# Thirteen transposes per head instead of fifteen: a new order of 64-blocks in the raw q/k tiles of an attention-and-mixing kernel

## The chip, the cores and the metric

One core of one Trainium2 chip runs the whole program. The metric is device time in microseconds (us), as the median of three runs. A profile of one further execution gives the trace from which all rows below are taken.

## The reference, cut to what matters

```python
B, H, S, D = 4, 8, 576, 64            # 32 heads of 576 positions, 64 wide
scores = (1 / sqrt(D)) * q @ k.T      # float32
cum    = cumsum(maximum(s, 0.0))      # one row of 576 per head
bias   = -(cum[:, None] - cum[None, :])
scores = where(causal, -1e9, scores + minimum(bias, 0.0))
attn   = softmax(scores)
x      = attn @ v                     # heads side by side: (4, 576, 512)
gate   = sigmoid(causal convolution of x, 5 taps)
x      = (gate * (x @ w_val)) @ w_out
h      = relu(x @ w_in);  u, v = halves of h, 512 wide each
v_n    = layer norm of v
out    = (u * (w_spatial @ v_n + b_spatial)) @ w_out2
```

q, k, v and s are float32; the weights come as 64-bit floats and are converted on the chip.

## The kernel before, in words

**Heads.** The main loop (L678 to L718) runs over rounds `w` of 0 to 32. Round `w` computes the scores of head `w`, turns the exponentials of head `w-1` and, when `w` is even, multiplies the pair of heads `w-2` and `w-1` with their values (`pv`). The first 8 heads (`NATIVE`) use plain float32 matmuls for the scores; the later ones split q and k into a high and a low part (`prep`) and use the faster float32r form.

**Scores.** The 576 queries of a head are cut into five tiles: 64 queries (positions 0 to 63) and four of 128. Tile `i` is scored against the keys up to its last query, so it has 64, 192, 320, 448 or 576 columns (`QE`). `scores` puts a tile's product in a PSUM bank; VectorE adds the mask and takes the row minimum of the negated scores (L219, into `p[i]`); ScalarE takes the exponential in place and sums the rows (L224). The last tile exceeds a bank of 512 columns and is cut into 288 and 288. Each of the five tiles has an SBUF tile of its own, `p[0]` to `p[4]`, and there are two sets.

**Turns.** The product with the values needs the exponentials with the keys on the partitions, so TensorE turns blocks of 128 queries by 128 keys with an identity as the moving operand (L271), into banks of up to five turns, and ScalarE copies each bank to `PT` (L272). There are 15 blocks on or under the diagonal; five of them, the last of each query tile (`c == i`), hold only 64 keys, and their turn fills half of its 128 columns' worth. The banks are `BANKS[0]` to `BANKS[3]` with 5, 1, 4 and 5 turns, and a round turns them in the order 1, 2, 3, 0 (L691, L699, L704).

**Values.** `pv` multiplies both heads of a pair; each head's product stands on its own 64 partitions of the bank. The six products of a head take 448, 448, 320, 192, 64 and 128 columns, 1600 in all. VectorE scales the result by the reciprocal row sums (L300), which were turned, written to DRAM and read back spread over partitions (`lay_sums`, `spread_sums`). `conv` then forms the gate's input.

**Mixing.** Beside the heads a queue of generators (`more`) feeds in weight conversion (`from_f64`, `weight_prep`, `fold_prep`), the folding of two weights, and the mixing stages of batches already attended. `n_g` sets how much of it each round takes, in five portions. The mixing of the last batch stands alone after the last head.

**Transfers.** All loads are issued from SP's queue, in the order of its instructions; an instruction that waits holds those behind it. `load(h)` brings q and k of a head (one transfer, L147 for the first 8 heads, L150 for the others), for the first 8 heads the row `cum` (L148), and the values (L152). `raw` has two buffers, `vraw` four. The same queue loads weights (L369, L471), the `cum` rows of the later heads (L168), a copy of q (L170) and the row sums (L248).

**Order.** The order of instructions on each engine is drawn up by the framework's planner from the program order and its own estimates; only a few places are pinned by hand.

Of the kernel before, what the change touches and what calls it, by code (L numbers as in the profile page):

```python
# [15 lines left out]
NEG = -1.0e30  # L16
# [8 lines left out]
def tile_stickbreak_attention_moe(  # L25
# [30 lines left out]
    BANKS = [[(4, 4), (1, 1), (1, 2), (1, 3), (1, 4)], [(0, 0)], [(0, 1), (0, 2), (0, 3), (0, 4)],  # L56
             [(2, 2), (2, 3), (2, 4), (3, 3), (3, 4)]]
    BLK, w = {}, 0
    for bank in BANKS:
        for c, i in bank:  # L60
            BLK[c, i] = w
            w += 64 if c == i else 128
    PTW = w
# [28 lines left out]
    V.memset(RAW[0][64:65, 0, :], 1.0)  # L92
    G.memset(RAW[1][64:], 0.0)
    G.memset(RAW[1][64:65, 0, :], 1.0)
# [6 lines left out]
    for c in (0, 128):  # L101
# [3 lines left out]
    mask = early.tile([128, S], F32, name="mask")  # L105
    G.memset(mask, 0.0)
    G.affine_select(out=mask[:, S - 128:], in_=mask[:, S - 128:], compare_op=ALU.is_ge, fill=NEG,
                    base=0, pattern=[[-1, 128]], channel_multiplier=1)
# [11 lines left out]
    for j in range(2):  # L120
        P.append([early.tile([128, e + 64], F32, name=f"p{j}{i}") for i, e in enumerate(QE)])
        for t, e in zip(P[j], QE):
            G.memset(t[:, e:], 0.0)
        G.memset(P[j][0][64:], 0.0)
# [16 lines left out]
    def load(h, cum=None):  # L141
        if h >= NH:
            return
        raw[h] = r = RAW[h % 2]
        src = qk2[h].rearrange("p (t s) -> p t s", t=2)
# [10 lines left out]
    def prep(h):  # L156

        if h >= NH:
            return
        r = raw.pop(h)  # L160
        if h < NATIVE:
            st[h] = r
            return
        qk = early.tile([128, 2, S], F32R, tag="qk", name="qk", bufs=2)
        kd = kds[h % 2]
        qc = cn[h % 2]
        qa, kb = qk[:, 0, :], qk[:, 1, :]
        SY.dma_start(f(kd[64:66]), cum_d[h])  # L168
        hi_of(A, qa, r[:, 0, :])
        SY.dma_start(f(qc[0:64]), f(qa[0:64]))  # L170
        lo_of(V, qa[64:128], r[64:128, 0, :], qa[64:128])
        hi_of(A, kb, r[:, 1, :])
        lo_of(V, kd[0:64], r[0:64, 1, :], kb[0:64])
        st[h] = (qa, kb, qc, kd)
# [15 lines left out]
    def scores(h, tiles):  # L190
        if h >= NATIVE:
            qa, kb, qc, kd = st[h]
        p = P[h % 2]
        if h not in NM:
            NM[h] = early.tile([128, 6], F32, tag="nm", name="nm", bufs=2)
        nm = NM[h]
        parts = []
        pst = None
        o = 0
        for i in tiles:  # L200
            q0, m, e = QS[i], QM[i], QE[i]
            spans = [(0, e)] if e <= 512 else [(0, HS), (HS, e)]
            for a, b in spans:
                if pst is None or o + b - a > 512 or len(spans) > 1:
                    pst = room("s", "pss", h)
                    o = 0
                if h < NATIVE:
                    r = st[h]
                    T.matmul(pst[0:m, o:o + b - a], r[:, 0, q0:q0 + m], r[:, 1, a:b], start=True, stop=True)  # L209
                else:  # L210
                    T.matmul(pst[0:m, o:o + b - a], qa[:, q0:q0 + m], kb[:, a:b], start=True, stop=False)  # L211
                    T.matmul(pst[0:m, o:o + b - a], qc[0:KD, q0:q0 + m], kd[0:KD, a:b], start=False, stop=True)  # L212
                parts.append((i, pst[0:m, o:o + b - a], a, b, len(spans)))
                o += b - a
        for i, src, a, b, n in parts:
            m, e = QM[i], QE[i]
            last = b == e
            o = S - max(e, 128) + a
            LAST["V"] = V.tensor_tensor_reduce(  # L219
                out=p[i][0:m, a:b], in0=src, in1=mask[0:m, o:o + b - a], scale=-0.125,  # L220
                scalar=3.0e38 if a == 0 else nm[0:m, 5:6], op0=ALU.add, op1=ALU.min,
                accum_out=nm[0:m, i:i + 1] if last else nm[0:m, 5:6])
            if last:
                A.activation(p[i][0:m, 0:e], p[i][0:m, 0:e], AF.Exp, bias=nm[0:m, i:i + 1], scale=-1.0,  # L224
                             accum_out=sm[h // 2 % 2][0:m, h % 2, i:i + 1])
# [31 lines left out]
    def transposes(h, tiles):  # L257

        p = P[h % 2]
        if h not in PT:  # L260
            PT[h] = early.tile([128, PTW], F32, tag="pt", name="pt", bufs=2)
        for bank in tiles:
            o0 = BLK[BANKS[bank][0]]
            pt = room("t", "pst", h)
            for c, i in BANKS[bank]:
                o = BLK[c, i]
                end = o + (64 if c == i else 128)


                r = 64 if c == i > 0 else 0  # L270
                T.transpose(pt[:, o - o0:o - o0 + 128], p[i][:, c * 128:(c + 1) * 128], ident[:, r:r + 128])  # L271
            A.activation(PT[h][:, o0:end], pt[:, 0:end - o0], AF.Copy)  # L272
# [3 lines left out]
    def pv(h):  # L276
# [3 lines left out]
        r = R.pop(h // 2).rearrange("p i q -> p (i q)")  # L280
        pts = [PT.pop(h + j) for j in range(2)]
        vs = [vraw.pop(h + j) for j in range(2)]

        first = None
        for tag, q0, q1 in (("o", 128, S), ("q", 0, 128)):
            po = ps.tile([128, 512], F32, tag=tag, name=f"ps{tag}", bufs=1)
            cs = [1, 0, 2, 3, 4] if q0 else [0]
            for c in cs:
                a = max(q0, c * 128)
                o = BLK[c, c] + a - c * 128  # L290
                for j in (1, 0):
                    with ExitStack() as es:
                        if first is not None:
                            es.enter_context(tc.issue_after(first))
                        m = T.matmul(po[64 * j:64 * j + 64, a - q0:q1 - q0], vs[j][:, c, :], pts[j][:, o:o + q1 - a],  # L295
                                     start=c == cs[0], stop=c == cs[-1])
                    first = first or m.ins
            for a, e in ((q0, 64), (64, q1)) if q0 == 0 else ((q0, q1),):
                o = a + 64 if a else 0
                V.tensor_tensor(out=x[:, a:e], in0=po[:, a - q0:e - q0], in1=r[:, o:o + e - a], op=ALU.mult)  # L300
# [22 lines left out]
    V.tensor_tensor_scan(out=cum, data0=s_sb, data1=s_sb, initial=0.0, op0=ALU.add, op1=ALU.max)  # L323
# [354 lines left out]
    for w in range(NH + 1):  # L678
# [11 lines left out]
        if w > 0:  # L690
            transposes(w - 1, [1, 2])  # L691
# [6 lines left out]
        if w > 0:  # L698
            transposes(w - 1, [3])  # L699
# [3 lines left out]
        if w > 0:  # L703
            transposes(w - 1, [0])  # L704
# [71 lines left out]
```

## Time and profile before

| | |
|---|---|
| median of 3 runs | 520.51 us (520.43 to 523.75) |
| the profiled execution | 523.57 us |
| its span, first to last instruction | 521.8 us |
| mean granted TensorE clock | 0.977 of full speed |
| TensorE matmul busy | 492.2 us, 94% of the span |
| ScalarE, VectorE busy | 339.3 us, 316.9 us |

The profiled execution's time is its span and 1.8 us around it. It stands 3.06 us above the median. PE is TensorE's matmul stream, PEld its weight loads, DVE VectorE, ACT ScalarE, POOL GpSimd, SP the queue of transfers. A matmul's recorded duration overlaps that of the next, so the step from one to the next is read from starts.

### The profile page before, as it was taken

The page shows a single profiled execution, that of the slowest core. Times are in us where ns is not written, and L with a number is a line of the kernel's source. Part 1 is how long each engine was busy: PE and PEld are TensorE (multiplying, and loading weights), DVE is VectorE, ACT ScalarE, POOL GpSimd, SP SyncE. Part 2 cuts the span into 40 slices and gives each one's busy share as a digit, 9 for nine tenths or more (in the row PEclk, how much of TensorE's full clock was granted, in tenths as well). Part 3 has the DMA queues.
Part 4 walks back from the last instruction along what each step waited for, and adds up shares of the span by engine and source line. Part 5 has one row for each costly group of instructions (what it writes and reads, how often), then busy time and mean ns, then how long its engine had stood idle before and what let it go on. Part 6 is the DMA issues. An engine that isn't in the chain of part 4 may idle for free.

```text
span 521.8 us, 9108 instructions
## 1 busy us (share of the span) xinstructions
PE 492.2 (94%) x3202; PEld 416.1 (80%) x3202; DVE 316.9 (61%) x834; ACT 339.3 (65%) x819; POOL 127.6 (24%) x167
## 2 busy tenths in 40 slices
PE   7889798989999999899999999999998999999997
PEld 5456564878769888889949889888878888998997
DVE  6778799788888684733748456744876526025120
ACT  3997797797687775864537647795869644224322
POOL 5212120036350103102235013003233013046140
PEclk9889798999999999989999999999998999999999
DMA  7839845356751643266511302666500052800002
GB/s 210 272 101 263 282 152 193 107 179 213 231 187 41 196 136 109 65 218 208 171 57 38 128 26 84 179 217 186 176 26 15 26 202 77 241 2 1 1 2 90
DMA packets 28302, 69.26 MB, mean 133 GB/s; under 512 B 4000, under 2 KB 12352, under 8 KB 28256
## 3 DMA queue, kind: packets, MB, share of 16 engines
q1 hardware_dynamic: 23328, 63.88, 39.7%
q10 hardware_dynamic: 4928, 4.80, 2.7%
q8 instruction: 25, 0.41, 0.3%
q14 instruction: 21, 0.17, 0.1%
HBM read 55.96 MB, written 9.16 MB: 125 GB/s over the span
## 4 chain that ended last, share of the span: by engine, by line
PE 65%; DVE 14%; DMA 10%; ACT 7%; issue 3%; SPq 1%; POOL 1%; ACTq 0%; DVEq 0%; POOLq 0%
PE psm L409 11%; PE psm L411 11%; PE psm L410 11%; PE pso L295 7%; PE pst L271 6%; PE psm L581 3%; DVE p L219 3%; PE psm L583 3%; PE psm L582 3%; PE pss L211 2%; DVE z L312 2%; PE pss L212 2%; DMA wr<-in_w_out 2%; PE pss L209 2%; DMA wv<-wo_d 1%
## 5 line engine op out<-in xcount | busy, mean ns | idle before, releaser
L224 ACT ACTIVATE p<-p,nm 64x64 f32<-64x64 f32 (+4 forms) x160 | 88.5, 555 | 10.5 <-DVE nm L219 10.0
L271 PE MATMUL pst<-ident,p 128*128 128x128 f32 x480 | 83.1, 284 | 7.3 <-ACT pt L272 3.8
L272 ACT ACTIVATE pt<-pst 128x512 f32<-128x512 f32 (+1 forms) x128 | 61.4, 496 | 34.2 <-PE psq L295 19.9
L219 DVE CUSTOM_DVE_ANT_0 p<-pss,mask 64x64 f32<-64x64 f32 (+4 forms) x160 | 64.1, 419 | 23.7 <-PE pss L212 17.1
L271 PEld LDWEIGHTS pst<-ident,p 128*128 128x128 f32 x480 | 61.5, 146 | 19.3 <-ACT pt L272 5.3
L312 DVE SCALAR_TENSOR_TENSOR z<-x,cw,z 128x575 f32<-128x575 f32 (+1 forms) x64 | 57.1, 892 | 6.2 <-ACT z L309 5.6
L79 POOL TENSOR_TENSOR g<-gt,g 128x288 fp32r<-128x288 f32 x32 | 29.2, 918 | 127.5 <-ACT g L72 95.2
L79 POOL TENSOR_TENSOR y<-gt,y 128x288 fp32r<-128x288 f32 x32 | 27.6, 867 | 111.1 <-ACT y L72 111.1
L295 PE MATMUL pso<-pt,vraw 128*64 128x448 f32 (+3 forms) x320 | 51.0, 431 | 1.2 <-ACT pt L272 1.2
L211 PE MATMUL pss<-qk 128*64 128x64 f32 (+1 forms) x144 | 45.2, 334 | 1.6 <-DVE nm L219 1.4
L295 PEld LDWEIGHTS pso<-pt,vraw 128*64 128x64 f32 x320 | 22.9, 139 | 27.0 <-issue 19.4
L212 PE MATMUL pss<-kd,cn 66*64 66x64 f32 (+1 forms) x144 | 42.1, 299 | 1.1 <-DVE kd L79 1.1
L209 PE MATMUL pss<-raw 128*128 128x288 f32 (+4 forms) x96 | 33.6, 453 | 7.0 <-DVE nm L219 5.3
L409 PE MATMUL psm<-g,wch 128*128 128x288 f32 x128 | 39.0, 310 | 0.2 <-ACT v L533 0.2
L581 PE MATMUL psm<-wsh,vh 128*128 128x288 f32 x128 | 38.5, 305 | 0.6 <-DVE gt L486 0.6
L411 PE MATMUL psm<-g,wch 128*128 128x288 f32 x128 | 38.5, 305 | 0.0
L410 PE MATMUL psm<-g,wcl 128*128 128x288 f32 x128 | 38.1, 302 | 0.0
L582 PE MATMUL psm<-wsh,vl 128*128 128x288 f32 x128 | 37.6, 298 | 0.0
L583 PE MATMUL psm<-wsl,vh 128*128 128x288 f32 x128 | 37.6, 297 | 0.0
L486 DVE TENSOR_TENSOR gt<-psm,u 128x288 f32<-128x288 f32 x32 | 14.4, 455 | 35.0 <-PE psm L585 22.1
L486 DVE TENSOR_TENSOR gt<-psm,z 128x288 f32<-128x288 f32 x32 | 14.4, 453 | 31.8 <-PE psm L411 29.2
L409 PE MATMUL psm<-y,wv 128*128 128x288 f32 x96 | 29.7, 310 | 3.8 <-ACT ot L596 2.9
(166 smaller groups left out, 1330.8 us busy)
## 6 DMA issues: line engine op xcount, KB each, us to landing
raw<-in_qk SPq DMA_DIRECT2D x24, 576.0 KB
wv<-wv_d SPq DMA_DIRECT2D x12, 512.0 KB
wv<-wo_d SPq DMA_DIRECT2D x12, 512.0 KB
vraw<-in_vp SPq DMA_DIRECT2D x32, 160.0 KB
R<-r_d SPq DMA_DIRECT2D x32, 160.0 KB
out<-ot ACTq DMA_DIRECT2D x32, 144.0 KB
cn<-qk SPq DMA_DIRECT2D x24, 144.0 KB
wr<-in_w_in SPq DMA_DIRECT2D x5, 512.0 KB
```

The lines of the kernel that those rows point to most:

```text
L79: eng.tensor_tensor(out=out_, in0=in_, in1=f(hi), op=ALU.subtract)
L211: T.matmul(pst[0:m, o:o + b - a], qa[:, q0:q0 + m], kb[:, a:b], start=True, stop=False)
L219: LAST["V"] = V.tensor_tensor_reduce(out=p[i][0:m, a:b], in0=src, in1=mask[0:m, o:o + b - a], scale=-0.125, scalar=3.0e38 if a == 0 else n ...
L224: A.activation(p[i][0:m, 0:e], p[i][0:m, 0:e], AF.Exp, bias=nm[0:m, i:i + 1], scale=-1.0, accum_out=sm[h // 2 % 2][0:m, h % 2, i:i + 1])
L271: T.transpose(pt[:, o - o0:o - o0 + 128], p[i][:, c * 128:(c + 1) * 128], ident[:, r:r + 128])
L272: A.activation(PT[h][:, o0:end], pt[:, 0:end - o0], AF.Copy)
L295: m = T.matmul(po[64 * j:64 * j + 64, a - q0:q1 - q0], vs[j][:, c, :], pts[j][:, o:o + q1 - a], start=c == cs[0], stop=c == cs[-1])
L312: V.scalar_tensor_tensor(out=z[:, d:], in0=x[:, :S - d], scalar=cw[:, p, k:k + 1], in1=z[:, d:], op0=ALU.mult, op1=ALU.add)
L409: T.matmul(pt, ah, bh, start=j == 0, stop=False)
L410: T.matmul(pt, al, bh, start=False, stop=False)
L411: T.matmul(pt, ah, bl, start=False, stop=j == n - 1)
L581: T.matmul(o, vh[c][:, cs], wsh[:, c, hs[hf]], start=c == 0, stop=False)
```

## The change

The keys of a head are laid in `raw` in another order: positions 512 to 575 first, then 0 to 511. The queries stand as 0 to 447, 512 to 575, 448 to 511. With it the five score tiles lie side by side in one SBUF tile of 1664 columns per set, and a half-filled block stands beside another half-filled block: the diagonal blocks of tiles 1 and 0 are turned together, and so are the last block of tile 3 and the first of tile 4. That leaves 13 turns per head, in four banks of 4, 4, 3 and 2.

What goes with it: `load` issues three transfers for q and k in place of one, in pieces of 1792, 256 and 256 bytes per row in place of one piece of 4608; the values come in two transfers, the second of which puts two blocks of 64 rows on the upper 64 partitions; the mask has 832 columns and four triangles instead of 576 and one; the scan that forms `cum` is cut in two; the last score tile is cut into 256 and 320; banks are turned in the order 3, 2, 0, 1; the value products take 512, 320, 192, 64, 448 and 64 columns, of which the two of 64 contract over the upper 64 partitions alone.

```diff
+    PO = [192, 0, 256, 640, 1088]
+    PW = 1664
+    MO = [384, 320, 192, 64, 0]
+    BANKS = [[(0, 0), (256, 0), (640, 0), (1152, 64)], [(128, 0), (384, 0), (768, 0), (1280, 64)],
+             [(512, 0), (896, 0), (1408, 64)], [(1024, 0), (1536, 64)]]
+    PTO = [(0, 0, 512), (512, 0, 512), (1024, 64, 320), (1344, 0, 256)]
...
-            SY.dma_start(r[0:64], src[0:64])
-            SY.dma_start(r[64:65, 1, :], one_d[h:h + 1] if cum is None else cum[h:h + 1])
-        else:
-            SY.dma_start(r, src)
-        vraw[h] = early.tile([128, 5, D], F32, tag="vraw", name="vraw", bufs=4)
-        SY.dma_start(vraw[h], vp[h].rearrange("p (c d) -> p c d", c=5))
+        by = r[0:n].rearrange("p t s -> p (t s)")
+        SY.dma_start(by[:, 64:1088].rearrange("p (t s) -> p t s", t=2)[:, :, 0:448], src[:, :, 0:448])
+        by = by.rearrange("p (g c) -> p g c", c=64)
+        SY.dma_start(by[:, 0:17:16], src[:, :, 512:])
+        SY.dma_start(by[:, 8:18:9], src[:, :, 448:512])
+        if h < NATIVE:
+            SY.dma_start(r[64:65, 0, :], one_d[h:h + 1] if cum is None else cum[h:h + 1])
+        vraw[h] = early.tile([128, 6, D], F32, tag="vraw", name="vraw", bufs=4)
+        vh = vp[h].rearrange("p (c d) -> p c d", c=5)
+        SY.dma_start(vraw[h][:, 0:4], vh[:, 0:4])
+        SY.dma_start(vraw[h][64:128, 4:], vh[0:64, 0::4])
...
-            spans = [(0, e)] if e <= 512 else [(0, HS), (HS, e)]
+            spans = [(0, e)] if e <= 512 else [(0, 256), (256, e)]
...
-            for c, i in BANKS[bank]:
...
-                T.transpose(pt[:, o - o0:o - o0 + 128], p[i][:, c * 128:(c + 1) * 128], ident[:, r:r + 128])
-            A.activation(PT[h][:, o0:end], pt[:, 0:end - o0], AF.Copy)
+            for t, (o, way) in enumerate(BANKS[bank]):
+                T.transpose(pt[:, 128 * t:128 * t + 128], p[:, o:o + 128], ident[:, way:way + 128])
+            to, o, n = PTO[bank]
+            A.activation(PT[h][:, to:to + n], pt[:, o:o + n], AF.Copy)
...
+        parts = [(0, 0, po), (2, 1024, po[:, 192:]), (3, 1408, po[:, 320:]), (4, 1344, po[:, 448:]),
+                 (1, 576, po[:, 64:]), (5, 512, pq)]
...
-    V.tensor_tensor_scan(out=cum, data0=s_sb, data1=s_sb, initial=0.0, op0=ALU.add, op1=ALU.max)
+    V.tensor_tensor_scan(out=cum[:, 64:], data0=s_sb[:, 0:512], data1=s_sb[:, 0:512], initial=0.0, op0=ALU.add, op1=ALU.max)
+    V.tensor_tensor_scan(out=cum[:, 0:64], data0=s_sb[:, 512:], data1=s_sb[:, 512:], initial=cum[:, S - 1:], op0=ALU.add,
+                         op1=ALU.max)
...
-            transposes(w - 1, [1, 2])
+            transposes(w - 1, [3, 2])
...
-            transposes(w - 1, [3])
+            transposes(w - 1, [0])
...
-            transposes(w - 1, [0])
+            transposes(w - 1, [1])
```

## Rows read from the trace of the kernel before

**Rows 1.** The page: busy time, share of span and instructions of each engine.

```profile
PE 492.2 (94%) x3202; PEld 416.1 (80%) x3202; DVE 316.9 (61%) x834; ACT 339.3 (65%) x819; POOL 127.6 (24%) x167
```

**Rows 2.** Busy time by stretch of the span, granted clock, DMA share and GB/s.

```profile
core 0: us, PE busy (x) PEld busy (x) DVE busy (x) ACT busy (x) POOL busy (x), PEclk, DMA share, GB/s
0.00:100.00 100.00, 85.13 (x425) 56.78 (x425) 81.20 (x232) 78.00 (x201) 23.39 (x40) 0.91 0.66 205
100.00:430.00 330.00, 319.64 (x2173) 275.38 (x2172) 210.88 (x558) 232.11 (x556) 77.47 (x92) 0.99 0.43 131
```

**Rows 3.** The chain that ended last, by line, whole span.

```profile
PE psm L409 11%; PE psm L411 11%; PE psm L410 11%; PE pso L295 7%; PE pst L271 6%; PE psm L581 3%; DVE p L219 3%; PE psm L583 3%; PE psm L582 3%; PE pss L211 2%; DVE z L312 2%; PE pss L212 2%; DMA wr<-in_w_out 2%; PE pss L209 2%; DMA wv<-wo_d 1%
```

**Rows 4.** Costliest groups, shapes apart: the turns; shares are busy us, mean ns.

```profile
L271 PE MATMUL pst<-ident,p 128*128 128x128 f32 x480 | 83.1, 284 | 7.3 <-ACT pt L272 3.8 <-ACT p L224 3.4
```

**Rows 5.** Timeline of PE: start, us from first start to last end, count.

```profile
228.31 0.71 PE L271 MATMUL pst<-ident,p 128*128 128x128 f32 x5
...
42.33 1.25 PE L271 MATMUL pst<-ident,p 128*128 128x128 f32 x10
...
62.04 2.13 PE L271 MATMUL pst<-ident,p 128*128 128x128 f32 x9
```

**Rows 6.** Busy time of line 271 alone, in two stretches.

```profile
0.00:100.00 100.00, 24.78 (x136) 18.97 (x136) 0.91 0.66 205
100.00:432.00 332.00, 58.28 (x344) 42.55 (x344) 0.99 0.43 133
```

**Rows 7.** Shapes apart: copies of turned banks, value products, last score tile.

```profile
L272 ACT ACTIVATE pt<-pst 128x512 f32<-128x512 f32 x96 | 55.0, 589 | 13.9 <-PE pst L271 12.4 <-ACT ot L596 0.4 <-PE pss L212 0.4
L272 ACT ACTIVATE pt<-pst 128x64 f32<-128x64 f32 x32 | 7.0, 218 | 20.3 <-PE psq L295 19.9 <-PE pst L271 0.4
...
L219 DVE CUSTOM_DVE_ANT_0 p<-pss,mask,nm 128x288 f32<-128x288 f32 x32 | 16.4, 511 | 14.0 <-PE pss L212 10.5 <-PE pss L209 2.5
L219 DVE CUSTOM_DVE_ANT_0 p<-pss,mask 128x288 f32<-128x288 f32 x32 | 14.3, 447 | 5.1 <-PE pss L212 4.8
```

**Rows 8.** Timeline of SP's queue at the start: each line an issue, its us.

```profile
1.18 0.55 SPq L147 DMA_DIRECT2D raw<-in_qk  x1
1.77 0.58 SPq L152 DMA_DIRECT2D vraw<-in_vp  x1
...
3.54 0.43 SPq L369 DMA_DIRECT2D wg<-in_conv_w  x1
4.01 0.44 SPq L369 DMA_DIRECT2D wg<-in_woT  x1
5.69 1.23 SPq L148 DMA_DIRECT2D raw<-cum  x2
...
7.59 0.31 SPq L335 DMA_DIRECT2D cum_d<-ch  x1
8.00 0.36 SPq L336 DMA_DIRECT2D cum_d<-cl  x1
8.41 0.42 SPq L152 DMA_DIRECT2D vraw<-in_vp  x1
```

**Rows 9.** The chain in order of time, first 10 us: start, us, what.

```profile
2.91 0.59 SPq L152
3.49 0.04 issue
3.54 4.08 DMA wg<-in_conv_w
```

**Rows 10.** Timeline of PE: the first scores, and the one stop for weights.

```profile
9.52 2.44 PE L209 MATMUL pss<-raw 128*64 128x64 f32 x8 [1.47 <-DMA raw<-cum]
...
230.71 0.37 PE L409 MATMUL psm<-y,wv 128*128 128x288 f32 x1 [0.94 <-DMA wv<-wo_d]
```

**Rows 11.** Timeline of SP's queue before that stop.

```profile
222.16 0.33 SPq L150 DMA_DIRECT2D raw<-in_qk  x1
223.44 0.32 SPq L471 DMA_DIRECT2D wv<-wo_d  x1
```

**Rows 12.** The page: DMA queues, packets, MB, share of 16 engines.

```profile
q1 hardware_dynamic: 23328, 63.88, 39.7%
q10 hardware_dynamic: 4928, 4.80, 2.7%
```

**Rows 13.** Line 271 alone: idle time of TensorE before it, us and times.

```profile
  ACT pt L272: 9.0, 8
  ACT p L224: 8.7, 9
```

**Rows 14.** Timeline of ACT and POOL, both writing tile g.

```profile
360.22 1.58 POOL L79 TENSOR_TENSOR g<-gt,g 128x288 fp32r<-128x288 f32 x2 [4.90 <-ACT g L72]
360.41 0.44 ACT L72 ACTIVATE g<-gt 128x288 fp32r<-128x288 f32 x1 [0.27 <-DVE gt L486]
```

**Rows 15.** The half-speed stretch of the turns at 62 us, all engines.

```profile
62.00:64.00 2.00, 2.00 (x11) 1.96 (x10) 2.00 (x6) 1.69 (x5) 1.04 (x1) 0.50 0.90 291
```

More of the change, by code (lines that the diff above doesn't have):

```diff
@@ L53, in tile_stickbreak_attention_moe @@
     QE = [64, 192, 320, 448, 576]
[L56 to L63, printed above, removed]
+    PO = [192, 0, 256, 640, 1088]
[4 more added lines that the diff above has]
+    PTO = [(0, 0, 512), (512, 0, 512), (1024, 64, 320), (1344, 0, 256)]
+    PTW = 1600
     V, G, A, T, SY = nc.vector, nc.gpsimd, nc.scalar, nc.tensor, nc.sync
@@ L104, in tile_stickbreak_attention_moe, with triangle @@
                         pattern=[[-1, n]], channel_multiplier=1)
-    mask = early.tile([128, S], F32, name="mask")
+    mask = early.tile([128, 832], F32, name="mask")
     G.memset(mask, 0.0)
-    G.affine_select(out=mask[:, S - 128:], in_=mask[:, S - 128:], compare_op=ALU.is_ge, fill=NEG,
-                    base=0, pattern=[[-1, 128]], channel_multiplier=1)
+    def triangle(t, base=0, row=1, col=-1):
+        G.affine_select(out=t, in_=t, compare_op=ALU.is_ge, fill=NEG, base=base, pattern=[[col, t.shape[1]]],
+                        channel_multiplier=row)
+    triangle(mask[:, 0:64])
+    triangle(mask[:, 0:64], 63, -1, 0)
+    triangle(mask[:, 384:512])
+    triangle(mask[64:, 768:])
     neghalf = early.tile([128, 1], F32, name="neghalf")
@@ L120, in tile_stickbreak_attention_moe @@
     for j in range(2):
[L121 to L124, printed above, removed]
+        P.append(early.tile([128, PW], F32, name=f"p{j}"))
+        G.memset(P[j][64:, 192:256], 0.0)
+        G.memset(P[j][:, 576:640], 0.0)
     mid = ctx.enter_context(tc.tile_pool(name="mid", bufs=1))
@@ L217, in scores @@
             last = b == e
-            o = S - max(e, 128) + a
+            o = MO[i] + (512 if a else 0)
+            row = p[0:m, PO[i]:PO[i] + e]
             LAST["V"] = V.tensor_tensor_reduce(
-                out=p[i][0:m, a:b], in0=src, in1=mask[0:m, o:o + b - a], scale=-0.125,
+                out=row[:, a:b], in0=src, in1=mask[0:m, o:o + b - a], scale=-0.125,
                 scalar=3.0e38 if a == 0 else nm[0:m, 5:6], op0=ALU.add, op1=ALU.min,
@@ L223, in scores @@
             if last:
-                A.activation(p[i][0:m, 0:e], p[i][0:m, 0:e], AF.Exp, bias=nm[0:m, i:i + 1], scale=-1.0,
+                A.activation(row, row, AF.Exp, bias=nm[0:m, i:i + 1], scale=-1.0,
                              accum_out=sm[h // 2 % 2][0:m, h % 2, i:i + 1])
@@ L284, in pv @@
         first = None
[L285 to L300, printed above, removed]
+        for c, o, to in parts:
+            k0 = 64 if c > 3 else 0
+            for j in (1, 0):
+                with ExitStack() as es:
+                    if first is not None:
+                        es.enter_context(tc.issue_after(first))
+                    m = T.matmul(to[64 * j:64 * j + 64], vs[j][k0:, 4 + (c == 4) if c > 3 else c, :],
+                                 pts[j][k0:, o:o + to.shape[1]], start=c in (0, 5), stop=c in (1, 5))
+                first = first or m.ins
@@ L302, in tile_stickbreak_attention_moe @@
+        V.tensor_tensor(out=x[:, 64:448], in0=po[:, 0:384], in1=r[:, 1:4].rearrange("p i q -> p (i q)"), op=ALU.mult)
+        xs, ps4, r4 = [t.rearrange("p (g c) -> p g c", g=2) for t in (x[:, 448:], po[:, 384:], r[:, 4])]
+        V.tensor_tensor(out=xs, in0=ps4, in1=r4[:, ::-1], op=ALU.mult)
+        V.tensor_tensor(out=x[:, 0:64], in0=pq, in1=r[:, 0, 0:64], op=ALU.mult)
     Z = {}
```

30 lines of the change are left out of this document (15 added, 15 removed).

## The prediction

> **What bounds the kernel now.** I read the engine totals first. TensorE's matmuls are busy for 492.2 us, 94% of the span, and no other engine passes 65% [rows 1]. An average hides stages, so the table by stretch comes next. From 100 to 430 us TensorE is busy 319.6 of 330 us, while VectorE and ScalarE have a third of their time free: there a matmul removed should be time removed. In the first 100 us TensorE has 85, VectorE 81 and ScalarE 78 us, and the DMA engines are at 0.66: several chains share that stage, and none alone sets it [rows 2]. After 430 us no head is left, so nothing of the change lies there. Third, the chain that ended last: the turns (L271) are 6% of it [rows 3], about 31 us.
>
> **The change, part by part.**
>
> *The removed turns.* 64 of 480 turns go. Their group shows 284 ns of busy time for one [rows 4], which would make 18.2 us. I don't use that figure: records of successive matmuls overlap. Ten turns in a row at full clock take 1.25 us and five take 0.71, so one more costs (1.25 - 0.71) / 5 = 0.108 us [rows 5]. Nine turns at the 0.50 clock [rows 15] take 2.13 us, 0.24 each with the last one's tail; twice 0.108 is 0.216.
>
> 136 of the turns lie in the first 100 us and 344 behind [rows 6]. Two fifteenths of them are 18.1 and 45.9. Behind 100 us that is 45.9 x 0.108 = 5.0 us. Before it the mean clock is 0.91, so about 18% of the time runs at half speed, and one turn costs about 0.108 x 1.18 = 0.127, together 2.3 us. The most that can be gained is 7.3 us. The chain gives the other bound: 2/15 of 31 us = 4.2. I take 4.7 for the late stage (97% of 5.0, TensorE's share of it) and half of 2.3, 1.1, for the early one where TensorE shares the bound: **-5.8 us**.
>
> The Trainium skill, "TensorE: Matmul & The Clock Gate", Part 4, gives about 275 ns for a 128x128 transpose in one kernel's context and says that the fast clock does not engage for it. The recorded duration here, 284 ns, agrees with that figure; the step of 0.108 and its doubling at the half clock speak against the rule as a price. By the duration the sum would be 12.4 us lower than mine; this is a rival below.
>
> *What stays equal.* The value products have 1600 columns per head before and after (448 + 448 + 320 + 192 + 64 + 128 against 512 + 320 + 192 + 64 + 448 + 64), six products each. Two contract over 64 rows, not 128; I know no row for that form and take no gain. ScalarE copies 1600 columns in four copies either way: from 218 ns for 64 columns and 589 for 512 [rows 7] a copy costs 165 ns plus 0.83 per column, four of them 1.99 us on both sides. The last score tile goes from 288 + 288 columns (0.447 + 0.511 us on VectorE [rows 7]) to 256 + 320: the same total. The masks are POOL's work ahead of the first scores, which wait for a transfer until 9.52 us [rows 10].
>
> *The copy's wait.* ScalarE stood 19.9 us before the small copy until the last value product released the buffer [rows 7]. The new order copies first into columns that earlier products read, so this may shrink. TensorE was busy in those times; I take 0, bound -1.5.
>
> *The transfers at the start.* Here the change costs. SP's queue is on the recorded chain from its first issues to the landing of `conv_w` [rows 9]. Two heads are loaded ahead of it; each gets two more q/k transfers and one more for the values, six more issues of 0.55 to 0.58 plus a gap of 0.04 [rows 8, 9]: 3.6 us. Queued behind them are `conv_w`, the first weights and the two `cum` rows. `conv_w` comes 3.6 us later. For the rows, SP had been free from 4.45 to 5.69 while VectorE formed `cum` [rows 8], so 1.2 us are absorbed and they go out 2.4 us later. The first scores stood 1.47 us for them [rows 10] and have no cover. VectorE then waits for scores and weights in turn. I take **+2.3 us**. Lower bound 0, if the planner puts the rows and weights ahead of the added pieces; upper bound 4.1, the 3.6 and one more value issue before the next weight load (L152 at 8.41 [rows 8]).
>
> *The transfers later on.* A later head gets the same three issues, at 0.33 each [rows 11], 1.0 us of SP's time per round. They load two rounds ahead. Behind them wait the weight loads of the mixing. One had no cover: `wv` was issued at 223.44, 1.3 us after `raw`, and TensorE stood 0.94 us for it [rows 10, 11]. There I charge half of 1.0, **+0.5 us**, bounds 0 and 1.0.
>
> The pieces themselves: a head has 640 more packets (256 of 1792 bytes and 512 of 256 for 128 of 4608). q1's packets average 142 ns at 2.74 kB, q10's 46 ns at 0.97 kB [rows 12], close to bytes alone. By bytes a 256-byte piece takes 13 ns and the total doesn't change; at q10's 46 ns each 512 of them are 23.6 us over 16 engines, 1.5 us per head, with the engines at 0.43 in the late stage [rows 2]. I take the lower end, as both rows follow bytes, and keep 1.0 us in the range. The Trainium skill, "DMA: Bandwidth & Descriptors", Specifications, asks for at least 512 bytes and says that smaller writes become read-modify-write. No row here has a 256-byte piece; the rule speaks against this change, and its weight would be the 1.5 us per head, under the same cover.
>
> *Sum.* -5.8 + 2.3 + 0.5 = -3.0. The profiled execution goes from 523.57 to 520.6. It ran 3.06 us above the median; as the terms are differences, they go over unchanged: 520.51 - 3.0 = **517.5 us**, 0.6% faster. Under about 1% (5.2 us) a measurement of this kernel hardly tells a change from none.
>
> **The rivals.**
>
> *The start costs nothing and every turn counts (faster).* If the planner keeps the `cum` rows and `conv_w` ahead of the second pieces, the start and later terms vanish, and all 7.3 us show: 513.2. With the copy's wait too, 511.7. For it: 97% TensorE, and an order drawn up anew. Against it: the planner already put both heads' q/k and value loads ahead of the `cum` rows [rows 8].
>
> *A turn costs its duration (much faster).* 64 x 0.284 = 18.2 in place of 5.8: 505.1. The step between starts contradicts it [rows 5]; kept as a rest.
>
> *The first bank waits for the last exponential (slower).* The change reverses what is turned first. Before, a round's first bank was the one small turn of tile 0, and tile 4 was first needed by the fourth turn of the next bank. Now the first bank needs tiles 3 and 4 of the head whose scores have just been made; their VectorE and ScalarE steps end last. Four turns of cover go, 0.43 us at full clock and 0.86 at half. TensorE already stood nine times, 8.7 us, before a turn for an exponential [rows 13]. If only those nine rounds are hit it is 4 to 8 us: 521 to 525. If all 32 are hit, 8 early ones at 0.86 and 24 at 0.43, it is 17 us: 534. It decides from the point where the wait hits about 17 rounds: then slower than 525.7. Against it: from round 9 on mixing work lies between, which the planner can move in front.
>
> *The parts don't stay independent (the change doesn't do what it says).* Five score tiles now share one SBUF tile, and three transfers write interleaved parts of one `raw`. If the framework orders them, a transfer waits for the landing of the one before, some 4.1 us [rows 9]: four such waits at the start, 16 less 1.2 us absorbed, put the end at 520.5 - 5.8 + 15.2 = 530. Against it: ACT writes one part of `g` at 360.41 while POOL writes another part from 360.22 on [rows 14], and the two interleaved halves of `cum_d` were issued 0.41 us apart, with no landing between [rows 8].
>
> **How the numbers follow.** My forecast has 0.45, the free start 0.32, the turn at full duration 0.03, the first bank 0.13 (slower by over 1% in rather more than half of it), the dependent parts 0.07. Forecast and first bank's mild form make "within 1%"; a little of the forecast's upper gain reaches "faster". That is 0.36 faster, 0.46 within, 0.18 slower. The range runs from 510.5, the free start with the copy's wait and a microsecond of new order, to 525.5, the first bank in its mild form; outside lie the full duration, the dependent parts and the first bank's worse half, about 0.18.
>
> **What the new profile would show.** 416 turns at an unchanged step, and some 18 us less busy time of L271 for a gain far below that. SP's first `conv_w` issue near 7.1 us and the first scores near 11.9, not 9.52; if they start at 9.5, the start was free. TensorE's idle time before L271 for an exponential above 8.7 us would show the first bank's wait; an SP issue of a second `raw` piece only after the first has landed, the dependence. The small copy's 19.9 us wait should be nearly gone. What would make me wrong: a different order on TensorE that opens or closes gaps of several microseconds, which no row of before can price.

## The result

The changed kernel takes 517.02 us (median of 20 runs, 513.98 to 522.67), the kernel before 522.51 us in the 20 runs beside it: a ratio of 0.9905, with a 95% interval of 0.9885 to 0.9925. That is 5.0 us, 0.95% faster; the ratio leaves out one run of the changed kernel that fell in a slower state. 517.5 was forecast, 3.0 us below the 520.51 of the first three runs. The time agrees better than the gain does: in these 20 runs the kernel before is itself 2.0 us slower than in those three. The gain came out larger than forecast, and four of the terms that make it were off, as the experiments show.

The profile page of the changed kernel, engine totals and two queues [rows 1, 12], the chain by line [rows 3], and the groups of turns, copies and value products [rows 4, 7]:

```profile
span 513.9 us, 9133 instructions
PE 481.8 (94%) x3138; PEld 402.4 (78%) x3138; DVE 315.6 (61%) x835; ACT 338.5 (66%) x819; POOL 128.3 (25%) x162
...
q1 hardware_dynamic: 46880, 63.88, 42.2%
q10 hardware_dynamic: 4928, 4.80, 2.8%
...
PE psm L420 9%; PE psm L421 9%; PE psm L422 9%; PE pso L303 5%; PE pst L279 4%; PE psm L592 3%; PE psm L594 2%; PE psm L593 2%; PE pss L224 2%; DMA out<-ot 2%; PE pss L225 2%; DMA wv<-wv_d 1%; ACT L238 1%; PE psm L595 1%; PE psm L596 1%
...
L279 PE MATMUL pst<-ident,p 128*128 128x128 f32 x416 | 64.3, 281 | 3.2 <-ACT p L238 3.2
L303 PE MATMUL pso<-pt,vraw 128*64 128x512 f32 (+4 forms) x320 | 54.0, 446 | 0.1
```

The turns (now L279) show 18.8 us less busy time than [rows 4]; the span is 7.9 us shorter, TensorE's idle time (span less busy) 32.1 us against 29.6. The table by stretch, answering to [rows 2], hardly changes from 100 us on; in the first 100 us TensorE is busy for 82.3 us, not 85.1:

```profile
0.00:100.00 100.00, 82.32 (x402) 52.80 (x402) 80.36 (x229) 76.44 (x197) 22.69 (x35) 0.93 0.69 204
100.00:430.00 330.00, 319.46 (x2185) 273.03 (x2186) 215.36 (x570) 236.00 (x568) 81.70 (x96) 1.00 0.45 134
```

The start is not the one that was priced. SP's queue [rows 8] in the timeline after (start, us, issue):

```profile
1.17 0.73 SPq L155 DMA_DIRECT2D raw<-in_qk  x1
1.95 0.60 SPq L157 DMA_DIRECT2D raw<-in_qk  x1
2.59 0.61 SPq L158 DMA_DIRECT2D raw<-in_qk  x1
...
6.14 0.61 SPq L160 DMA_DIRECT2D raw<-cum  x1
...
11.54 0.42 SPq L380 DMA_DIRECT2D wg<-in_conv_w  x1
```

And TensorE's first scores there [rows 10]:

```profile
8.25 1.36 PE L222 MATMUL pss<-raw 128*64 128x64 f32 x6
```

The planner put head 0's `cum` row ahead of head 1's later pieces, and `conv_w` behind the loads of both heads and the copies of `cum`: it goes out at 11.54 us, not 3.54, and the first scores start at 8.25, not 9.52. A later stop is new, for the row of head 2:

```profile
20.84 1.39 PE L222 MATMUL pss<-raw 128*64 128x64 f32 x4 [2.97 <-DMA raw<-one_d]
```

Before the turns, line 279 alone, TensorE's idle time for an exponential (us, times) [rows 13]:

```profile
  ACT p L238: 7.6, 8
```

Its one stop for weights, in the timeline, with SP's issue of the load that was the stop in [rows 10]. The stop is now for another load, `wv_d` and not `wo_d`:

```profile
222.36 0.54 SPq L482 DMA_DIRECT2D wv<-wo_d  x1
...
233.14 0.37 PE L420 MATMUL psm<-xvh,wv 128*128 128x288 f32 x1 [1.82 <-DMA wv<-wv_d]
```

Before the copies, line 281 alone, ScalarE's idle time and what ended it [rows 7]:

```profile
  PE pst L279: 24.3, 22
  PE psq L303: 4.3, 3
```

Turns in TensorE's timeline [rows 5]:

```profile
62.22 0.60 PE L279 MATMUL pst<-ident,p 128*128 128x128 f32 x4
...
228.38 1.04 PE L279 MATMUL pst<-ident,p 128*128 128x128 f32 x8
```

Four more turns take 0.44 us: the step is 0.110, as before.

### The profile page after: what moved, and what is told of

The parts are those of the page before. It is cut to its first block, busy times and chain, and to the rows that moved or that the text cites. A ratio compares the mean times of both kernels' runs of the same rounds, so it can differ in the third digit from the quotient of the medians.

```text
span 513.9 us, 9133 instructions
## 1 busy us (share of the span) xinstructions
PE 481.8 (94%) x3138; PEld 402.4 (78%) x3138; DVE 315.6 (61%) x835; ACT 338.5 (66%) x819; POOL 128.3 (25%) x162
## 4 chain that ended last, share of the span: by engine, by line
PE 49%; ACT 3%; DMA 3%; issue 1%; DVE 1%; ACTq 0%; DVEq 0%
PE psm L420 9%; PE psm L421 9%; PE psm L422 9%; PE pso L303 5%; PE pst L279 4%; PE psm L592 3%; PE psm L594 2%; PE psm L593 2%; PE pss L224 2%; DMA out<-ot 2%; PE pss L225 2%; DMA wv<-wv_d 1%; ACT L238 1%; PE psm L595 1%; PE psm L596 1%
## 5 line engine op out<-in xcount | busy, mean ns | idle before, releaser
L281 ACT ACTIVATE pt<-pst 128x512 f32<-128x512 f32 (+2 forms) x128 | 60.2, 498 | 30.0 <-PE pst L279 24.3
L233 DVE CUSTOM_DVE_ANT_0 p<-pss,mask 64x64 f32<-64x64 f32 (+4 forms) x160 | 63.0, 413 | 19.3 <-PE pss L225 8.5
L279 PE MATMUL pst<-ident,p 128*128 128x128 f32 x416 | 64.3, 281 | 3.2 <-ACT p L238 3.2
L279 PEld LDWEIGHTS pst<-ident,p 128*128 128x128 f32 x416 | 51.2, 145 | 10.9 <-ACT p L238 4.5
L321 DVE SCALAR_TENSOR_TENSOR z<-x,cw,z 128x575 f32<-128x575 f32 (+1 forms) x64 | 55.2, 863 | 7.1 <-ACT z L318 6.6
L303 PE MATMUL pso<-pt,vraw 128*64 128x512 f32 (+4 forms) x320 | 54.0, 446 | 0.1
L224 PE MATMUL pss<-qk 128*64 128x64 f32 (+1 forms) x144 | 43.6, 321 | 1.8 <-ACT pt L281 1.2
L222 PE MATMUL pss<-raw 128*128 128x320 f32 (+4 forms) x96 | 32.2, 448 | 8.6 <-DVE nm L233 5.3
L420 PE MATMUL psm<-g,wch 128*128 128x288 f32 x128 | 38.4, 304 | 1.3 <-ACT v L544 1.3
L303 PEld LDWEIGHTS pso<-pt,vraw 128*64 128x64 f32 (+1 forms) x320 | 19.5, 137 | 25.3 <-issue 17.6
L422 PE MATMUL psm<-g,wch 128*128 128x288 f32 x128 | 37.5, 297 | 0.0
```

The source lines that it names most:

```text
L224: T.matmul(pst[0:m, o:o + b - a], qa[:, q0:q0 + m], kb[:, k0 + a:k0 + b], start=True, stop=False)
L233: LAST["V"] = V.tensor_tensor_reduce(out=row[:, a:b], in0=src, in1=mask[0:m, o:o + b - a], scale=-0.125, scalar=3.0e38 if a == 0 else nm[0 ...
L279: T.transpose(pt[:, 128 * t:128 * t + 128], p[:, o:o + 128], ident[:, way:way + 128])
L281: A.activation(PT[h][:, to:to + n], pt[:, o:o + n], AF.Copy)
L303: m = T.matmul(to[64 * j:64 * j + 64], vs[j][k0:, 4 + (c == 4) if c > 3 else c, :], pts[j][k0:, o:o + to.shape[1]], start=c in (0, 5), sto ...
L321: V.scalar_tensor_tensor(out=z[:, d:], in0=x[:, :S - d], scalar=cw[:, p, k:k + 1], in1=z[:, d:], op0=ALU.mult, op1=ALU.add)
```

## The experiments

Three questions were open: what a turn is worth at the end, what the transfers cost, and what else moved. Each ratio below is against the kernel before, timed on the same chip; 0.001 is 0.52 us. The changed kernel was not timed again beside them: its 0.9905 is carried over. The theory was the prediction's sum; the rivals were a dearer or free turn, free transfers, and an order of instructions that makes the difference.

**Planner's own order.** Four kernels vary one part each and let the planner order them anew.

```diff
 e1: bank 3 turned twice (15 turns per head); e2: four times (19)
+            for _ in range(2 if bank == 3 else 1):          # e2: range(4 ...)
-            for t, (o, way) in enumerate(BANKS[bank]):
+                for t, (o, way) in enumerate(BANKS[bank]):
...
 e3: the kernel before, q and k in three transfers, values in two
+            for c, e in ((0, 448), (448, 512), (512, S)):
+                SY.dma_start(r[:, :, c:e], src[:, :, c:e])
...
 e4: the changed kernel, tensors laid beforehand, one transfer each
+        SY.dma_start(r[0:n], qk2[h].rearrange("p (t s) -> p t s", t=2)[0:n])
...
+        SY.dma_start(vraw[h], vp[h].rearrange("p (c d) -> p c d", c=6))
```

> The changed kernel with the two turns of its last bank made twice: 15 turns per head again, everything else as changed; the second pair writes the same values to the same place. Theory (a turn costs its step of 0.108 us where TensorE sets the pace): the 64 turns come back at 5.8 us, bounds 4.2 and 7.3, so the ratio to the kernel before goes from 0.9905 to about 1.002 (0.999 to 1.005). Rival A (the gain of the change came from another order and fewer half-speed stretches, the turns were hidden): no change from 0.9905 within 0.3%. Rival B (a turn costs its recorded duration, 0.28 us): 18 us more, ratio 1.025. The busy time of the turns in the trace should go up by about 18 us under any of them.

> The changed kernel with the two turns of its last bank made four times: 19 turns per head. 192 turns more than the changed kernel. Theory: 0.09 us each on the path, 17.4 us more, ratio to the kernel before 1.024 (12.6 to 21.9 us, 1.015 to 1.033). Rival A: within 0.3% of the changed kernel's 0.9905. Rival B (0.28 us each): 54 us more, ratio 1.095. Against the run with two more it gives the slope free of what a new order does once.

> The kernel before with the transfers alone cut as in the change: q and k of a head in three transfers of 448, 64 and 64 columns to their old places, the values in two (four chunks and one). 15 turns, old order of keys, nothing else touched. Theory: the six added issues ahead of the first weights cost 2.3 us at the start and 0.5 later, ratio 1.005 (0 to 5.1 us, 1.000 to 1.010); the first weight load is issued 3.6 us later or more. Rival A (the transfers are hidden everywhere): ratio 1.000 within 0.2%. Rival B (small pieces load the DMA engines): 1.5 us per head in stages without cover, ratio above 1.02, and the DMA share goes up by a tenth or more.

> The changed kernel with q, k and values laid out in the new order in DRAM beforehand, so that one transfer brings q and k and one the values, as in the kernel before; the turns, the masks, the order of banks and the products are the changed kernel's. Theory: the 2.8 us of the transfers come back, so 5.8 us faster than the kernel before plus what the copy's wait gave: ratio 0.989 to 0.985, that is 0.002 to 0.006 below the changed kernel's 0.9905; the first weight load is issued near 3.5 us as before. Rival A (transfers hidden): 0.9905 within 0.2%. Rival C (the late first weight load of the changed kernel, at 11.54 us, helped by letting the first heads ahead): slower than the changed kernel.

Measured: e1 1.0205 (1.017 to 1.024), e2 1.0256 (1.0215 to 1.0298), e3 1.0033 (1.0008 to 1.0057), e4 1.0041 (1.0008 to 1.0074). Read as prices these contradict each other: two turns more per head would cost 15.7 us, four more on top only 2.7; and taking transfers away (e4) would cost 7.1. What they share is a new order on every engine. So in the next four that order was taken out: each engine's instructions are held in the sequence of the changed kernel (q1 to q3) or of the kernel before (q4), and an added instruction stands right behind the one written before it.

> The changed kernel with the two turns of its last bank made twice, as in the run with two more, but with the order of instructions on all five engines fixed to that of the changed kernel; the added turns stand right behind their originals. Theory 1 (a turn costs 0.09 us on the path; what the earlier run paid beyond that was its new order): 5.8 us more than the changed kernel, ratio to the kernel before 0.9905 + 0.011 = 1.002 (0.998 to 1.005). Theory 2 (the turns themselves carry the 15.7 us of the earlier run): ratio 1.0205 again. Theory 3 (turns hidden, all of the change's gain is order): 0.9905 within 0.3%.

> The changed kernel with the two turns of its last bank made four times (192 more turns), order of all engines fixed to the changed kernel's. Theory 1: 0.09 to 0.108 us each, 17 to 21 us more, ratio 1.024 to 1.030. Theory 2: the slope between two and six more in the planner's own orders, 128 turns for 2.6 us, 0.02 us each, would give only some 4 us over the run with two more. Theory 3: 0.9905 within 0.3%.

> The changed kernel with q, k and values laid out in DRAM beforehand and brought by one transfer each, with the order of all five engines fixed to the changed kernel's; the dropped transfers leave no gap. Theory 1 (the three transfers cost 0 to 3 us, and the 7 us by which the same layout in its own order was slower were that order): equal to the changed kernel or up to 3 us faster, ratio 0.985 to 0.991. Theory 2 (early landing of the heads or the weights by single transfers is itself harmful): 1.004 again.

> The kernel before with q and k in three transfers and the values in two, to their old places, with the order of all five engines fixed to that of the kernel before; each added issue stands right behind its first piece, so that all ten stand ahead of the first weights and of the cum rows. Theory 1 (the start as I worked it out): first weight load 3.6 us later, first scores 2.4 us later, ratio 1.0055 (1.000 to 1.010). Rival (hidden): 1.000 within 0.2%, though the first scores start 2 us late. In its own order this cut measured 1.0033.

Measured: q1 0.997 (0.9943 to 0.9996), q2 1.0131 (1.0095 to 1.0168), q3 0.987 (0.983 to 0.9911), q4 1.0139 (1.0101 to 1.0178). Against the changed kernel's 0.9905 the 64 turns of q1 cost 0.0065, 3.4 us (1.7 to 5.1), and the 192 of q2 0.0226, 11.8 us (9.6 to 14.0): 0.053 and 0.061 us for one. Both ratios lie below what was expected. The same content in another order differs by 0.0235 (e1 and q1, 12.3 us), 0.0171 (e4 and q3, 8.9 us), 0.0125 (e2 and q2) and, the other way round, 0.0106 (e3 and q4): each more than the 64 turns are worth in a held order.

The engine totals tell part of why a turn is worth about half its step. q1's page:

```profile
span 516.4 us, 9260 instructions
...
PE 488.9 (95%) x3202; PEld 410.4 (79%) x3202; DVE 316.8 (61%) x835; ACT 339.1 (66%) x819; POOL 128.2 (25%) x162
```

q2's page:

```profile
span 526.4 us, 9518 instructions
...
PE 498.5 (95%) x3330; PEld 420.9 (80%) x3330; DVE 316.2 (60%) x835; ACT 338.9 (64%) x819; POOL 132.5 (25%) x162
```

64 turns add 7.1 us of TensorE's busy time, 0.111 each, which is the step; but its idle time falls from 32.1 to 27.5 us. 192 add 16.7, 0.087 each, and idle time is 27.9. So some 4 us of the added turns fall where TensorE waits anyway, no more of them with 192 than with 64.

Another part goes with the granted clock, which none of these runs holds. Its mean over the runs is 0.983 in the changed kernel, 0.985 in q1 and 0.991 in q2; in the profiled executions it is 0.987, 0.986 and 0.994. Among the runs of the kernel before in each of the three groups of experiments, a clock higher by 0.01 goes with a time shorter by 2.3 to 2.9 us. By that, an estimate, q2 would take 2 to 2.5 us more at the clock of the changed kernel. No run separates waits from clock.

In q4, with the order of before, SP's queue at the start, in its timeline:

```profile
7.24 0.43 SPq L377 DMA_DIRECT2D wg<-in_conv_w  x1
...
8.26 1.24 SPq L151 DMA_DIRECT2D raw<-cum  x2
```

And TensorE's first scores in q4:

```profile
11.41 2.94 PE L217 MATMUL pss<-raw 128*64 128x64 f32 x8 [3.28 <-DMA raw<-cum]
```

Both came out as the prediction had worked them: `conv_w` at 7.24 (forecast near 7.1), scores at 11.41 (near 11.9). The whole of q4 costs 0.0139, 7.3 us, more than the 1.010 at the top of what was expected. Left to the planner (e3), 1.7 us. Part of that difference can be the granted clock: 0.978 in the mean of q4's runs against 0.983 in the kernel before beside it, and 0.987 in e3's against 0.985. In the order of after the transfers cost 0.9905 - 0.987 = 0.0035, 1.8 us, with intervals that overlap.

**The value products over 64 rows.** The timeline showed a term without a price: blocks of value products took longer after the change. The theory was that TensorE loses time at each change between a product over 128 rows and one over 64; the rival, that the time lies beside a wait or in the small products themselves. Three kernels were made for it, and a fourth for the order alone (all with the order held):

```diff
 r1: after, all value products over 128 rows (lower rows of two value blocks zeroed per head)
-            k0 = 64 if c > 3 else 0
+            k0 = 0
+        G.memset(vraw[h][0:64, 4:], 0.0)        # in prep
 r2: after, the two products over 64 rows next to each other
-                 (4, 1344, po[:, 448:]), (1, 576, po[:, 64:]), (5, 512, pq)]
+                 (1, 576, po[:, 64:]), (4, 1344, po[:, 448:]), (5, 512, pq)]
 r4: before, its last product over the 64 rows that hold keys
+                n = 64 if c == 4 else 128
+                    m = T.matmul(..., vs[j][0:n, c, :], pts[j][0:n, o:o + q1 - a], ...)
 r3: after without its pieces: q1's 15 turns, q3's one transfer, r1's 128 rows (zeros laid beforehand)
```

> The changed kernel with the order of its instructions on the five engines held, but the two half value products of each head contract over all 128 rows: the lower 64 rows of those values are zeroed by a memset on GpSimd for each head, 32 in all, which add zero. Theory (a change between a product over 128 rows and one over 64 costs TensorE about 0.1 us, because the weights of the next are not loaded ahead, four times for each pair of heads): the uninterrupted block of a pair falls from 3.30 us to near 2.85, 16 x 0.45 = 7.2 us are gained, 0.9905 falls to about 0.977. Rival (the longer block lies beside a wait that would be there anyway, or its length comes from the halves' own small tiles): 0.988 to 0.993.

> The changed kernel with its order held; only the fourth and the fifth part of a pair's value products change places, so that the four products over 64 rows stand next to each other: two changes of form for each pair in place of four, with the same products. Theory of the change of form: 16 x 2 x 0.1 = 3.2 us less, 0.9905 falls to about 0.984. Rival (each product over 64 rows is itself the dear one): the block stays at 3.30 us and the ratio at 0.9905.

> The kernel before with its order held; only its value product of the last 64 keys contracts over the 64 rows that hold keys, not over 128 of which 64 are zeros: two changes of form for each pair of heads, nothing else. Theory of the change of form: 16 x 0.2 = 3.2 us more, 1.006, and up to 1.014 if a change costs twice that here. Rival (products over fewer rows cost nothing): 1.000.

> What is left of the change when its pieces are taken out and its order on the engines is kept: 15 turns for each head (the two of the last bank made twice), one transfer for a head's queries and keys and one for its values (laid beforehand), all value products over 128 rows. The counts of turns, transfers and products are then those of the kernel before. Theory (about 10 us of the gain are the order in which the instructions stand on the engines, the start's transfers among them): 0.9870 (one transfer) + 0.0065 (two turns more) - 0.0138 (value products) = about 0.980. Rival (the order is worth nothing, and the pieces' costs add up otherwise): 1.000.

The last pair's block in TensorE's timeline, before (start, us from first start to last end, matmuls):

```profile
407.97 2.70 PE L295 MATMUL pso<-pt,vraw 128*64 128x448 f32 x20
410.50 0.39 PE L295 MATMUL psq<-pt,vraw 128*64 128x128 f32 x4
```

The same in after:

```profile
416.68 3.11 PE L303 MATMUL pso<-pt,vraw 128*64 128x512 f32 x20
419.72 0.33 PE L303 MATMUL psq<-pt,vraw 64*64 64x64 f32 x4
```

The same in r1:

```profile
417.57 2.81 PE L304 MATMUL pso<-pt,vraw 128*64 128x512 f32 x20
420.21 0.28 PE L304 MATMUL psq<-pt,vraw 128*64 128x64 f32 x4
```

The same in r2:

```profile
412.28 2.96 PE L303 MATMUL pso<-pt,vraw 128*64 128x512 f32 x20
415.07 0.28 PE L303 MATMUL psq<-pt,vraw 64*64 64x64 f32 x4
```

The same in r4:

```profile
405.62 2.85 PE L296 MATMUL pso<-pt,vraw 128*64 128x448 f32 x20
408.39 0.44 PE L296 MATMUL psq<-pt,vraw 128*64 128x128 f32 x4
```

Each head's value product runs as two matmuls, 24 for a pair, and the two heads' run beside each other: their records start 0.007 us apart. In that order (before, after, r1, r2, r4) the block takes, from first start to last end, 2.92, 3.37, 2.92, 3.07 and 3.21 us for the same 1600 columns per head. The changes between 128 and 64 rows inside it number 0, 3, 0, 1 and 2: each costs 0.15 us, whichever kernel it stands in, and the product itself nothing. The other undivided blocks, eight of 16 in before and r4 and seven in the other three, take the same to 0.01 us. So the change of form is shown. TensorE's weight loads show what happens there (timeline of PEld, after, then r1):

```profile
418.55 0.46 PEld L303 LDWEIGHTS pso<-pt,vraw 64*64 64x64 f32 x8 [0.28 <-issue]
...
418.48 1.12 PEld L304 LDWEIGHTS pso<-pt,vraw 128*64 128x64 f32 x14 [0.29 <-issue]
```

In after the weights of the first 64-row product are loaded from 418.55, when their own matmul starts; in r1 the loads of that product and the next run on from 418.48, ahead of their matmuls. Over 16 pairs the blocks would give 16 x 0.45 = 7.2 us of TensorE's time in the changed kernel. Nine of its pairs are divided by other work; eight of these take 0.29 to 0.45 us more than in r1, so some 6 us is nearer.

How much of it reaches the end is less clear. r2 gave 0.9856 (0.9816 to 0.9895): 2.6 us less than the changed kernel, with intervals that overlap, where the blocks give at most 16 x 0.30 = 4.8. r4 gave 1.0015 (0.9986 to 1.0044): 0.8 us, at most 2.3, where the blocks give at most 16 x 0.29 = 4.6 and the eight undivided ones alone 2.3; the expected 1.006 is excluded. r1 gave 0.989 (0.9844 to 0.9935), 0.8 us, and missed its 0.977. But its memsets may not have been free: GpSimd stood for the value products that still read the buffer, and what came behind on its queue stood with it. The memsets' group in r1 (busy us, mean ns, idle before and what ended it):

```profile
L173 POOL MEMSET vraw<- 64x128 f32 x32 | 7.3, 232 | 16.0 <-PE psq L304 11.1 <-PE pso L304 2.6 <-issue 1.5
```

TensorE's busy time in r1 is 477.2 us, 4.6 less than after, with a span of 514.0: its idle time rose from 32.1 to 36.8. No row shows that the memsets caused this, and the granted clock of its runs was lower too, 0.979 against 0.983. That run doesn't separate its two theories.

r3 gave 0.9815 (0.9776 to 0.9854); 0.980 was expected, the rival's 1.000 is excluded. With the counts of turns, transfers and value products of the kernel before, the layout and order of the changed one are worth 9.6 us (7.6 to 11.7). About 1 us of it goes with the granted clock (0.988 against 0.983), by the 2.8 us for 0.01 in the kernel before beside it. The table by stretch of the kernel before, TensorE alone (busy us, matmuls, granted clock, DMA share, GB/s):

```profile
100.00:200.00 100.00, 95.61 (x627) 1.00 0.51 160
200.00:300.00 100.00, 97.27 (x643) 0.98 0.41 126
260.00:280.00 20.00, 20.00 (x87) 1.00 0.18 54
300.00:430.00 130.00, 126.76 (x909) 0.99 0.37 113
```

The same of r3:

```profile
100.00:200.00 100.00, 96.14 (x627) 1.00 0.50 162
200.00:300.00 100.00, 98.03 (x703) 1.00 0.43 131
260.00:280.00 20.00, 20.00 (x129) 1.00 0.16 51
300.00:430.00 130.00, 125.69 (x899) 0.99 0.38 120
```

Both programs have 3202 matmuls. Up to 200 us both have done about as many; from 200 to 300 r3 does 60 more, with nearly the same busy time. So the gain there isn't idle time filled. Some of it is the clock: from 220 to 230 us before does 57 and r3 75, at a granted clock of 0.83 against 1.00. From 260 to 280 both are busy throughout at the full clock, and r3 does 42 more: there matmuls follow each other faster. That place shows how. There the planner dealt a pair's value products out, one by one, between mixing matmuls (TensorE's timeline, before):

```profile
262.03 0.97 PE L295 MATMUL pso<-pt,vraw 128*64 128x448 f32 x4
262.94 0.50 PE L409 MATMUL psm<-wch,g 128*128 128x512 f32 x1
...
263.98 0.39 PE L410 MATMUL psm<-wch,g 128*128 128x512 f32 x1
264.21 0.40 PE L411 MATMUL psm<-wcl,g 128*128 128x512 f32 x1
264.53 0.97 PE L295 MATMUL pso<-pt,vraw 128*64 128x448 f32 x2
265.43 0.49 PE L409 MATMUL psm<-wch,g 128*128 128x512 f32 x1
265.86 0.96 PE L295 MATMUL pso<-pt,vraw 128*64 128x448 f32 x2
266.75 0.49 PE L410 MATMUL psm<-wch,g 128*128 128x512 f32 x1
```

At 262.03 the products of both heads, side by side, take 0.91 us to the next start; at 264.53 one head's product alone takes 0.90. So a product that is dealt out alone loses the run beside the other head's. One value product (two matmuls) and one mixing matmul take 1.33 us (264.53 to 265.86). A mixing matmul among its own kind takes 0.23 us (263.98 to 264.21); two matmuls of 448 columns take 0.41 at the rate of the undivided block (2.92 us for 2 x 2 x 1600 columns). So about 0.7 us are lost per cycle, with TensorE shown busy throughout. The changed kernel's order and r3's hold the blocks together more often: counted over the traces, the value products of the 16 pairs stand in 41 unbroken stretches in before and in 31 in every kernel with the order of after. Where two runs have the same content, the one with more stretches was the slower each time: e1 49 and q1 31, e4 44 and q3 31, e2 40 and q2 31, q4 41 and e3 38. This is argued from the trace; no run changes the dealing out alone, and it explains only part of the 9.6 us.

## Why the prediction was right, and where it was not

The sum was -5.8 + 2.3 + 0.5 = -3.0 us; -5.0 was measured (0.0095 x 522), with an interval of 0.2% to either side, so a change under 1% can be told from none. By the held orders it is made of other parts:

| part | forecast, us | measured, us | from |
|---|---|---|---|
| 64 turns fewer | -5.8 | -3.4 (-1.7 to -5.1), -3.9 (-3.2 to -4.7) | q1, q2 |
| transfers, start and later | +2.8 | +1.8, interval reaches 0 | q3 |
| value products over 64 rows | 0 | +0.8 to +6.2, see below | r1, r2, r4; remainder |
| order and layout | 0 | -9.6 (-7.6 to -11.7) | r3 |

The remainder: 0.9815 (r3) - 0.0065 + 0.0035 leaves 0.9785; the changed kernel stands at 0.9905, so the form would be 0.0120, 6.2 us, if the parts add up; with it the sum closes by construction. The direct runs found 0.8 to 2.6. Which it is stays open.

*The turns.* The price was right: 0.111 us of TensorE for one (q1), unchanged step, 18.8 us less recorded busy time for a far smaller gain. The size of the term was off: the step that failed is "97% of 5.0, TensorE's share of it". (97% of 5.0 is also 4.8 or 4.9 rather than 4.7.) A stage that is 97% busy didn't pass on 97% of what was added: some 4 us fell into TensorE's waits, and the granted clock was higher in the kernels with more turns. The bound that the chain gave, 4.2, was the nearer one. q1 and q2 add turns to the last bank, not where the change took them away; that the place makes no difference is not shown. The rival at the full duration (505.1) is out. The rule of the Trainium skill, "TensorE: Matmul & The Clock Gate", Part 4, is no price here: the duration agrees with it, the step doesn't.

*The transfers at the start.* The arithmetic was right for the order that it assumed: q4 is that order, and shows 7.24 and 11.41. The step that failed is taking the order as given. The rival of the free start had the mechanism half right: the `cum` row went ahead, but `conv_w` did not stay ahead, it went behind. The start was not free either: TensorE stood 2.97 us at 20.84 us for a head's row. That stop belongs to the order and not to the pieces, since q3, with one transfer for each head in the same order, has one of 2.87 us at 19.18. How badly a queue's order can price this is seen in q4, 7.3 us for pieces that cost 1.7 in e3. There `conv_w` goes out 3.7 us later (7.24 against 3.54) and the first scores start 1.9 us later; how much of either reaches the end, and where the rest arises, no run shows.

*The transfers later on.* The stop that was charged did not come: the planner sent `wo_d` at 222.36, ahead of the next `raw` at 223.74, and TensorE did not wait for it. Another load, `wv_d`, stopped it for 1.82 us in this profile and for 0.22 in that of the run q1, in the same order; so the step that failed is again the order taken as given. The 256-byte pieces: the share of queue q1 in 16 engines over the span is 0.422 x 513.9 = 216.9 us against 0.397 x 521.8 = 207.2, so 9.7 us over 32 heads, 0.3 per head, between the ends of 0 and 1.5. The trace of after has 18432 packets of 256 bytes, at 18 ns each in the mean, where 13 by bytes and 46 by queue q10 were the two ends. The weight that I had worked out for the rule of the Trainium skill, "DMA: Bandwidth & Descriptors", Specifications, was five times what was measured. The count of 640 more packets for each head was low: there are 23552 more in all, 736 per head, as the values are in smaller pieces too.

*The value products.* "I know no row for that form and take no gain" was the step that failed: a cost was as possible as a gain, and the term had no bound on either side. The prediction counted columns and products; the changes between forms were what cost.

*The copy's wait* went from 19.9 us [rows 7] to 4.3, as forecast, with waits for the turns themselves up to 24.3; no gain at the end was claimed, and none was tested. *The first bank's wait* did not come: 7.6 us in 8 places against 8.7 in 9 [rows 13]. (Its threshold of about 17 rounds does not follow from its own prices: the 8.2 us up to 525.7 are 11 rounds if the eight at 0.86 are among them, 19 at 0.43 alone.) *The parts of one `raw` stayed independent*: its three issues stand at 1.17, 1.95 and 2.59 us, with no landing between. Nothing here shows the same of the shared score tile.

*The order* was named as what would make the prediction wrong, and given no price. It is the largest term of the four, and happened to stand against the unpriced value products. The forecast's closeness is in part that cancellation, and in part the 2.0 us between the two medians of the kernel before: both are luck.

## What to carry to other kernels

Where a planner redraws the order, hold the order before a part of a change is priced: the same instructions moved by 5.5 to 12 us here, more than most parts. On an engine that is 97% busy a removed step is worth less than its time (here about half), since some of the steps fill waits and the granted clock moved with the number of steps; add steps at a held order and read busy time, idle time and granted clock. Look in the planner's order for products that stand alone where two could run side by side. Count changes between matmul forms, not only columns: r2 puts the two short products side by side with one line and stands at 0.9856, not told apart from the changed kernel's 0.9905. r3's order and full-row products with 13 turns would come to about 0.9815 - 0.0065 = 0.975 by these prices, an estimate that was not run.

## What the runs showed of the hardware

A change between matmuls over 128 and over 64 rows cost 0.15 us in the blocks above, alike in three kernels, with no idle time of the matmuls shown. Value products of two heads ran beside each other, and one alone took as long as the two (0.90 against 0.91 us); one dealt out between mixing matmuls lost about 0.7 us. Packets of 256 bytes took 18 ns. A group's busy time isn't the price of its members: 480 turns show 83.1 us in the kernel before [rows 4] and 71.7 in r3, whose group is

```profile
L273 PE MATMUL pst<-ident,p 128*128 128x128 f32 x480 | 71.7, 281 | 2.1 <-ACT p L231 2.0
```
